# A gated attention and MLP mix on one Trainium2 core: another hand-written order of the attention, a shared PSUM pair for adjacent PV groups, and four small moves

## The chip, the cores and the metric

The kernel runs on one core of one Trainium2 chip. The metric is the device time of one execution in microseconds (us). The core has five engines that the text names as the profile does: TensorE (PE for its matmuls, PEld for its weight loads), VectorE (DVE), ScalarE (ACT), GpSimd (POOL) and SyncE (SP). Each works through its own queue in program order. DMAs are issued from the queues of SyncE and ScalarE here. Matmul results land in PSUM, which the kernel handles as banks of 128 x 512 float32 values, eight of them.

## The reference

The input x has 2048 rows of 512 values. Two branches work on it, and a gate mixes them:

```python
def _A_ref(x, wqkv, wo):                 # attention: 32 heads of 16, window of 256 keys
    qkv = (x @ wqkv) ...                 # q, k, v per head
    scores = einsum("bhqd,bhkd->bhqk", q, k) * (16 ** -0.5)
    mask = (q_index - k_index >= 0) & (q_index - k_index < 256)
    p = softmax(where(mask, scores, -1e9))
    return einsum("bhqk,bhkd->bhqd", p, v) ... @ wo

def _B_ref(x, w1, b1, w2, b2):           # channel MLP: 512 -> 1792 -> 512
    y = layernorm(x)
    h = gelu(y @ w1 + b1)
    return h @ w2 + b2

g = sigmoid((x * gate_w).sum(-1, keepdims=True))
out = g * _A_ref(x, ...) + (1 - g) * _B_ref(x, ...)
```

## The kernel before

Everything is float32. For the large products each operand is split into a rounded high part (type fp32r) and the rest, its low part; the product is then three matmuls, high times high, high times low and low times high. A high part is a copy or cast to fp32r (helper `copy` on ScalarE, line 131, or a VectorE `tensor_copy`), a low part is a subtraction (helper `lo_part`, line 128, on VectorE or GpSimd).

The kernel has three stages, one after the other on TensorE.

**Head and projections (to about 144 us).** `first_units` (line 259) computes the first q and k projection in four steps of 128 input values each. In a step both weight tiles, `ws[0]` and `ws[1]`, are cast to a high part and subtracted to a low part, the x chunk is split by `hi` and `lo`, and six matmuls (line 290) use them. `load_x(c)` (line 232) returns these helpers for one of the four chunks of x; `lo` uses VectorE for chunks 0 to 2 and GpSimd for chunk 3. Then a list of units follows (`qk_unit`, line 297, with its matmuls at line 303, and `v_unit`, line 326, matmuls at line 333), with a plan of what else is issued at which unit. q and k go to DRAM and come back as stacks of heads. The first rows of scores for the maxima (`s_pair`) run here too.

**Attention and the MLP's first layer (about 144 to 488 us).** Four kinds of work are woven together by the string ORDER, a letter at a time, in `run` (line 735):

- S (`s_pair`, line 348): two score matmuls (line 357) into a PSUM pair; VectorE masks them (line 366) and takes each row's maximum (line 367). After every fourth row block `put_max` (line 371) sends the maxima through DRAM into extra rows of the q stack. Its four steps run 6, 13, 19 and 28 letters after the S (`CHAIN`); the third, `put` (line 385), issues a DMA from ScalarE's queue, or from SyncE's for the maxima that are finished before ORDER starts.
- T (`st_pair`, line 403): two transposed score matmuls (line 412), which include the subtracted maximum; ScalarE takes the exponential (line 414) and GpSimd zeroes what the mask excludes (line 416).
- P (`pv`, line 423): up to 16 matmuls of a PV group (line 431) in four column tiles of 32, into the first bank of a PSUM pair. ScalarE copies the result out (VectorE once no S is left).
- f (`fill`, line 706): one step of the MLP's first layer (`mlp1_unit`, line 626): two matmuls (line 638) with 64 rows each. 24 steps make one unit, which holds one PSUM pair all that time; its two banks are copied out by ScalarE at the end.

The eight PSUM banks are four pairs, b0 to b3, in a list `ring`. `two` (line 112) takes the pair for the next T, S or P from it: the place in the list is a digit of the string PICK, 0 being the pair that was used longest ago. A pair may be written again when its last reader is done. After ORDER come six more fills, the last P and the remaining fills.

**Second layer and output (about 488 us to the end).** A loop over 4 chunks of 512 rows x 14 blocks of the hidden layer runs `mlp2` (line 851, matmuls at line 858), 12 matmuls a step. `attn_out(c)` (line 794) is called at step 4 for the first chunk and at step 11 of each chunk for the next one. With `after(k, ...)`, which puts work k steps later, it loads the attention's sums, takes reciprocals (line 810), loads the numerators and the reciprocals, and from the tenth step on scales one block of 128 rows a step (`scale`, line 815: a VectorE product at line 816, a high and a low part); a step later 12 matmuls (line 827) multiply it by wo.

Of the kernel before, what the change touches and what calls it, by code (L numbers as in the profile page):

```python
# [34 lines left out]
EPS = 1e-5  # L35
NEG = -3.0e38
U8 = mybir.dt.uint8
ORDER = ("TfSfSfffffTfSfffTSfffTfSfffTSfffTfSffSPTSffTfSfffTSfffSPSTfSfffTfSfTffTffTSffTfffTSPSSTPSTfTfffTSffT"
         "ffSffTSffffTSfffTfSffTfSfffSPSTSPTffSTffTfffTfSTffffTSffTfSfffTSfffTfSffSPSSTPTffTSffTffSffTfSfffTSf"
         "ffTfSfffTSfffTfSfSPSTTPTTSPSSTPSffTSffffSTfffTffSffTfSfffTfSffTfSfffSPSTTffffSTffTfffSTffTfffSSPfSfT"  # L40
         "ffSffTfTfffTSPSSTPTffTSfffTfSffTfSffffTSfffTfSffTffSffTPfSSPTffSfTfSffTfSfTffTffSTfffSffTfSfffTSfffS"
         "PTSTPSTSPTffTSffTffSffTSffffTSffffSTfffTffTfSfSfPSSTPfSfTfSfffTfTffSfTfSffffTSfffTfSffffTfSPSTSPTfSf"
         "ffTSfffTfSffTfSfffTfSfTfffTSfTffffTSPTTSPSTSPfTfSTfffSfffTSfffTfSffTfSfffTSfffTfSffSPPSTffTfffSTffTf"
         "ffTfSTfffSfTffTfSffTfSfffSPSSTPSffTfSfffTSfffTfSfffTSfffTfSfffTSffffSPPfSTfTfffSfTffTfSffTffTfSffTff"
         "SfTfTffffSPTTSPSTSPSfffTSfffTfSffTfSffffTSfffTfSffTfSfffSPfSTfTffffTfSTfffTfSfffTSfffTfSffTfSfffSPTS"
         "SPPTSTffffTfSTfffSffTfSfffTSfffTfSffTfffSfSPTSTPSSfTffffTfSffTfSfffTSfffTfSfffTSfffffSTPTTSPTSffTffS"
         "ffTfSfffTSfffTffSfTfTfffSTfTfffSPSSSPPSTSffffTfSfffTSfffTfTfffSTfffTffSTffffSPSTSPSTffTfffSTffTffTSf"
         "ffSffTSfffTfSffTfSfffSPSTSPfTfSTfffTffTSfffTfSfffTSfffTfSffTfSfffSPTTSPSTSPTffTSffTfSfffTfSfffSSfffT"
         "ffffTSffTfSffSPSffTSfffTfSffTfSffSTfffTffTffTfTffffTfPPTTTPfTffTffTffTPPTfTfffTffTfffTTffTfffTfPfTTf"
         "TTffffP")  # L50
PICK = ("0000000000000000001000000000000000000001000100100000000000000000100001000100000000000001000000000000"
        "0000000000000100010000010000000000001001001000101010001000100000000000000000001000000000100000000000"
        "0010000000000001000010020101010000000000100101000000000000000010000001000010000000000000000100100010"
        "1000000000100000000000000000000000000000000000000001000000000000000000010001000000000000001000000100"
        "0000000000000000100000000000000000000000000001001100000010010000000010010000000010000010000000000010"
        "00010000000000000000000101000100000100000000000000010000000000000000000000000000000")
LAG = 6
CHAIN = (6, 13, 19, 28)

# [2 lines left out]
def gated_mix_kernel(ctx, tc: tile.TileContext, xt, x2, wq0, wqk, wv, wo, xa, gw, w1, w2, b1, b2, out):  # L62
# [67 lines left out]
    def copy(dst, src):  # L130
        act.activation(dst, src, AF.Copy)  # L131
# [12 lines left out]
    spot = [None]  # L144
# [87 lines left out]
    def load_x(c):  # L232
        h, l = x8(), x8()
        xh.append(h)
        xl.append(l)
        raw = vs[:, 4 * c:4 * c + 4].rearrange("p b r -> p (b r)")
        for dt in range(DT):
            sp.dma_start(raw[:, dt * C:(dt + 1) * C], xt[c, :, dt * C:(dt + 1) * C])

        def part(t, dt):  # L240
            return t[:, dt * C:(dt + 1) * C]

        def hi(dt, eng=act):
            if eng is dve:
                dve.tensor_copy(part(h, dt), part(raw, dt))
            else:
                copy(part(h, dt), part(raw, dt))

        def lo(dt):
            lo_part(part(l, dt), part(raw, dt), part(h, dt), dve if c < 3 else pool)  # L250

        def rest():
            for dt in range(DT):
                hi(dt)
                lo(dt)

        return rest, hi, lo

    def first_units():
        ws, os = [], []  # L260
        for t in range(2):
            w = wt()
            wq[0, t] = w
            ws.append(w)
        raws = f32(get("work", "wv", DT, (128, 2, 512), F32R)).rearrange("p a (d t n) -> p (a d) t n", d=2, t=2)
        for a, b in ((0, 1), (1, 2), (2, 4)):
            act.dma_start(raws[:, a:b], wq0[:, a:b])
        _, hi, lo = load_x(0)
        idle = t2()
        dve.memset(idle[:, :256], 0.0)  # L270
        idle = idle.bitcast(BF16)
        o = two()[:, 0]
        for _ in range(10):
            pe.matmul(o, idle[:, :128], idle[:, :512], start=True, stop=True)
        loads()
        for t in range(2):
            os.append(ps("d"))
        for dt in range(DT):
            k = slice(dt * 128, dt * 128 + 128)
            if dt == 0:  # L280
                hi(dt, dve)
            for t in range(2):
                copy(ws[t][:, 0, k], raws[:, dt, t])
                lo_part(ws[t][:, 1, k], raws[:, dt, t], ws[t][:, 0, k])
                if dt and not t:
                    hi(dt)
            lo(dt)
            for n, (k, x) in enumerate(((0, xh[0]), (1, xh[0]), (0, xl[0]))):
                for t in range(2):
                    pe.matmul(os[t], ws[t][:, k, dt * 128:dt * 128 + 128], x[:, dt * C:dt * C + C],  # L290
                              start=dt == 0 and n == 0, stop=dt == DT - 1 and n == 2)
        rests[1]()
        rests[2]()
        for t in range(2):
            qk_out(0, t, 0, os[t])
# [75 lines left out]
    def put_max(p, a):  # L371
        mx = mxs[p][:, :, :, a:a + 4]
        m = small("nm", 2, (128, 2, 2, 2, 4), F32R)
        ms = small("ms", 2, (128, 32))
        md = dram.tile([2, 2, 2, 4, 128], F32R, name=nm("md"))

        def parts():
            pool.tensor_copy(m[:, 0], mx)
            lo_part(m[:, 1], mx, m[:, 0], pool)

        def turn():
            dve.transpose(ms, f32(m).rearrange("p a b c d -> p (a b c d)"))

        def put(eng=act):
            eng.dma_start(f32(view(md, [32, 4], [128, 32], [1, 32])), ms)

        def rest():
            done.add(("m", p, a // 4))
            for k in range(2):
                src = view(md, [512, 2], [1024, 2], [1, 512], off=2048 * k)  # L390
                sp.dma_start(f32(qk[62 + k:113 + k:50, :2, a * 128:a * 128 + 512]), f32(src))

        if spot[0] is None:
            parts()
            after(1, lambda: (turn(), put(sp)))
            after(3, rest)
        else:
            for n, fn in zip(CHAIN, (parts, turn, put, rest)):
                soon(n, fn)
# [19 lines left out]
    def flush():  # L419
        while late:  # L420
            late.pop(0)()

    def pv(p, j, last):
        flush()
        a = two()[:, 0]
        parts = ((-1, 0, 128, 256), (-2, 0, 256, 128), (0, 0, 0, 256), (1, 128, 0, 128))[0 if j else 2:]
        for n, (d, at, fr, w) in enumerate(parts):
            kb = 2 * j + d
            for h in range(4):
                v = (4 * p + h) * VW  # L430
                pe.matmul(a[32 * h:32 * h + 32, at:at + w], vs[:, kb, v:v + 32], pts[p, kb][:, h, fr:fr + w],  # L431
                          start=n == 0, stop=n == len(parts) - 1, skip_group_check=True, tile_position=(0, 32 * h))
        if j % 2 == 0:
            sums.append(sums.pop(0))
            acc[p] = sums[-1]
        s = acc[p]
        o = j % 2 * 256
        if last:
            dve.tensor_copy(s[:, o:o + 256], a[:, :256])
        else:  # L440
            copy(s[:, o:o + 256], a[:, :256])
        if j % 2:
            to = osc[p, :, (j - 1) * 256:(j + 1) * 256]
            if lt:
                after(1, lambda: sp.dma_start(to, s))
            else:
                act.dma_start(to, s)
# [287 lines left out]
    def run(order):  # L735
        for a in order:
            spot[0] += 1
            for fn in soons.pop(spot[0], []):
                fn()
            flush()  # L740
            if a == "T":
                p, kb, pr = lt.pop(0)
                if not pr:
                    block(p, kb)
                st_pair(p, kb, pr)
            elif a == "S":
                s_pair(*ls.pop(0))
            elif a == "P":
                pv(*lp.pop(0), not ls)
            else:  # L750
                fill()
# [42 lines left out]
    def attn_out(c):  # L794
# [49 lines left out]
                after(g, lambda g=g: load_o(g))  # L844
            after(4 + g, lambda g=g: load_r(g))
        for b in range(4):
            after(10 + b, lambda b=b: scale(b, *(t[:, :, b * 128:b * 128 + 128] for t in (o, r))))

    accs = {}

# [98 lines left out]
```

## Time and profile before

| what | value |
|---|---|
| median of 3 runs | 694.88 us |
| the three runs | 691.83, 694.88, 695.27 us |
| the profiled execution's own time | 691.57 us |
| its span (first to last instruction) | 689.8 us |
| granted TensorE clock | 1.00 |
| TensorE busy with matmuls | 681.9 us (99%) |
| VectorE, ScalarE, GpSimd busy | 474.1, 385.5, 267.2 us |

The profile is of one execution. The profiled execution's own time is 1.7 us more than its span. A row of the timeline reads: start in us, length in us, engine, line, operation, output <- input, shape, xcount, and in brackets the idle time of the engine before it with what ended it. In a group's row the numbers behind the bar are the busy time in us, the mean length of one in ns, and the idle time before them. A matmul's end is modelled; its start is not.

### The profile page before, as it was taken

The page shows a single profiled execution, that of the slowest core. Times are in us where ns is not written, and L with a number is a line of the kernel's source. Part 1 is how long each engine was busy: PE and PEld are TensorE (multiplying, and loading weights), DVE is VectorE, ACT ScalarE, POOL GpSimd, SP SyncE. Part 2 cuts the span into 40 slices and gives each one's busy share as a digit, 9 for nine tenths or more (in the row PEclk, how much of TensorE's full clock was granted, in tenths as well). Part 3 has the DMA queues.
Part 4 walks back from the last instruction along what each step waited for, and adds up shares of the span by engine and source line. Part 5 has one row for each costly group of instructions (what it writes and reads, how often), then busy time and mean ns, then how long its engine had stood idle before and what let it go on. Part 6 is the DMA issues. An engine that isn't in the chain of part 4 may idle for free.

```text
span 689.8 us, 15777 instructions
## 1 busy us (share of the span) xinstructions
PE 681.9 (99%) x5738; PEld 538.2 (78%) x5738; DVE 474.1 (69%) x971; ACT 385.5 (56%) x639; POOL 267.2 (39%) x623
## 2 busy tenths in 40 slices
PE   9999999999999999999999999999999999999997
PEld 6887777877877778778787877777787888888886
DVE  6646789966877878778587777866575555556444
ACT  6437454447677676876767767678633224123221
POOL 6900156426566664755666655558000000000000
PEclk9999999999999999999999999999999999999999
DMA  8998888785765668665776556436775450841801
GB/s 319 351 317 271 246 255 270 226 248 176 231 202 165 203 212 271 194 198 177 198 251 195 182 166 202 154 108 216 277 241 189 143 181 4 267 133 40 255 0 62
DMA packets 89621, 137.92 MB, mean 200 GB/s; under 512 B 13160, under 2 KB 36648, under 8 KB 89416
## 3 DMA queue, kind: packets, MB, share of 16 engines
q1 hardware_dynamic: 81120, 128.69, 58.4%
q10 hardware_dynamic: 8424, 8.23, 3.9%
q8 instruction: 46, 0.75, 0.5%
q14 instruction: 31, 0.25, 0.1%
HBM read 81.53 MB, written 54.30 MB: 197 GB/s over the span
## 4 chain that ended last, share of the span: by engine, by line
PE 86%; DMA 7%; POOL 3%; DVE 1%; ACT 1%; SPq 1%; issue 1%; ACTq 0%; DVEq 0%; POOLq 0%
PE ps_b L638 22%; PE ps_a L858 16%; PE ps_b L431 12%; PE ps_d L303 10%; PE ps_b L357 7%; PE ps_b L412 6%; PE ps_o L827 6%; PE ps_d L333 6%; DMA ra<-rd 1%; DMA hp<-t 1%; DMA t<-in_w 1%; DMA oa<-osc 1%; PE ps_x L357 1%; DMA wv<-in_wq 1%; POOL x L128 1%
## 5 line engine op out<-in xcount | busy, mean ns | idle before, releaser
L638 PE MATMUL ps_b<-x,w 64*128 64x512 f32 x1344 | 211.1, 395 | 0.2 <-ACT pb L414 0.2
L858 PE MATMUL ps_a<-x,t 128*128 128x512 f32 x648 | 149.6, 389 | 0.0
L367 DVE TENSOR_REDUCE mx<-ps_b 128x2 f32<-128x512 f32 x208 | 144.1, 693 | 7.2
L858 PEld LDWEIGHTS ps_a<-x,t 128*128 128x128 f32 x648 | 121.6, 188 | 25.3
L638 PEld LDWEIGHTS ps_b<-x,w 64*128 64x128 f32 x1344 | 130.0, 186 | 10.6 <-issue 2.0
L366 DVE COPY_PREDICATED ps_b<-tri,ps_b 128x256 f32<-128x256 uint8 x208 | 88.3, 424 | 44.0 <-PE ps_b L357 32.7
L416 POOL TENSOR_SCALAR_AFFINE_SELECT pa<-pa 128x256 f32<-128x256 f32 x192 | 73.9, 412 | 68.6 <-ACT pa L414 67.9
L414 ACT ACTIVATE pa<-ps_b 128x768 f32<-128x768 f32 x96 | 76.5, 813 | 25.6 <-PE ps_b L412 18.8
L412 PE MATMUL ps_b<-qk 64*128 64x384 f32 (+5 forms) x512 | 88.8, 336 | 0.4 <-ACT pb L414 0.3
L303 PE MATMUL ps_d<-x,w 128*128 128x512 f32 x360 | 85.1, 391 | 0.1
L357 PE MATMUL ps_b<-qk 62*128 62x384 f32 (+3 forms) x472 | 83.2, 345 | 0.8 <-ACT t L131 0.6
L303 PEld LDWEIGHTS ps_d<-x,w 128*128 128x128 f32 x360 | 67.2, 188 | 15.1 <-POOL x L128 0.5
L416 POOL TENSOR_SCALAR_AFFINE_SELECT pb<-pb 128x256 f32<-128x256 f32 x160 | 62.4, 417 | 39.2 <-ACT pb L414 38.5
L414 ACT ACTIVATE pb<-ps_b 128x768 f32<-128x768 f32 (+2 forms) x96 | 65.6, 706 | 16.8 <-PE ps_b L412 12.5
L412 PEld LDWEIGHTS ps_b<-qk 64*128 64x128 f32 (+1 forms) x512 | 50.8, 184 | 15.7 <-issue 4.0
L694 ACT ACTIVATE t<-t,b1s 128x512 f32<-128x512 f32 x56 | 38.5, 716 | 43.4 <-DMA t<-hp 42.8
L416 POOL TENSOR_SCALAR_AFFINE_SELECT x<-x 128x256 f32<-128x256 f32 x128 | 49.7, 417 | 25.8 <-ACT x L414 25.4
L357 PEld LDWEIGHTS ps_b<-qk 62*128 62x128 f32 (+1 forms) x472 | 45.4, 184 | 17.4 <-issue 3.8
L414 ACT ACTIVATE x<-ps_b 128x768 f32<-128x768 f32 x64 | 51.2, 813 | 13.0 <-PE ps_b L412 10.4
L827 PE MATMUL ps_o<-w,t 128*128 128x512 f32 x192 | 46.3, 390 | 1.0 <-ACT t L131 1.0
L333 PE MATMUL ps_d<-wv,x 128*128 128x512 f32 x192 | 46.7, 394 | 0.0
L431 PE MATMUL ps_b<-pa,v 128*32 128x256 f32 (+1 forms) x768 | 43.3, 330 | 0.2 <-POOL x L416 0.2
(96 smaller groups left out, 757.1 us busy)
## 6 DMA issues: line engine op xcount, KB each, us to landing
qk<-qk SPq DMA_DIRECT2D x112, 196.0 KB
t<-hp SPq DMA_DIRECT2D x56, 256.0 KB
hp<-t SPq DMA_DIRECT2D x54, 256.0 KB
qk<-t SPq DMA_DIRECT2D x48, 256.0 KB
osc<-x SPq DMA_DIRECT2D x31, 256.0 KB
t<-in_w SPq DMA_DIRECT2D x28, 256.0 KB
w<-w SPq DMA_DIRECT2D x28, 256.0 KB
qk<-t ACTq DMA_DIRECT2D x24, 256.0 KB
```

The costliest lines, as they stand in the source:

```text
L303: pe.matmul(o, a[:, dt * 128:(dt + 1) * 128], b[:, dt * C:(dt + 1) * C], start=n == 0, stop=n == 11)
L333: pe.matmul(o, x[:, a:a + 128], wvs[dt][:, k], start=n == 0, stop=n == 11)
L357: pe.matmul(o[:, e, :n], qs[pr][r:k, qb * 128:qb * 128 + 128], ks[pr][r:k, t0:t0 + n], start=True, stop=True)
L366: dve.copy_predicated(o[:, :, :128], tri, o[:, :, 256:384])
L367: dve.tensor_reduce(m, o[:, :, :256], mybir.AxisListType.X, ALU.max)
L412: pe.matmul(o[:, e, :w], ks[pr][r:k, kb * 128:kb * 128 + 128], qs[pr][r:k, kb * 128:kb * 128 + w], start=True, stop=True)
L414: act.activation(pt[:, :, :w], o[:, :, :w], AF.Exp, scale=0.25)
L416: pool.affine_select(out=pt[:, :, a:a + 128], in_=pt[:, :, a:a + 128], pattern=[[0, 2], [sgn, 128]], base=b, channel_multiplier=-sgn, comp ...
L431: pe.matmul(a[32 * h:32 * h + 32, at:at + w], vs[:, kb, v:v + 32], pts[p, kb][:, h, fr:fr + w], start=n == 0, stop=n == len(parts) - 1, sk ...
L638: pe.matmul(o[:, e], w[kt // 4][r:r + 64, k, m:m + 128], y[r:r + 64, a:a + C], start=n == 0, stop=n == 23)
L827: pe.matmul(a, x[:, g], wos[g][:, k], start=n == 0, stop=n == 11)
L858: pe.matmul(accs[c][b], x[:, b * 128:(b + 1) * 128], w, start=f == 0 and n == 0, stop=f == FT - 1 and n == 2)
```

## The change

Six edits:

- ORDER and PICK are replaced. The new ORDER has the same 256 T, 236 S and 63 P, and 647 f in place of 652; PICK has 575 digits in place of 583.
- `pv` takes a PSUM pair by `two` only if it has none open: a P right behind another P uses the second bank of the same pair. Any other letter between them closes the pair.
- `attn_out` starts its scaling at step 12 in place of 10 for the first chunk; the other chunks keep 10.
- In `first_units` the second weights' high parts of steps two to four are cast by VectorE, ahead of the step's other work, and no longer by ScalarE.
- The low parts of x chunk 3 are computed by VectorE for its last two tiles; GpSimd keeps the first two.
- `put` issues its DMA from SyncE's queue while the letter count `spot[0]` is at most 99, and from ScalarE's after that.

```diff
-ORDER = ("TfSfSfffffTfSfffTSfffTfSfffTSfffTfSffSPTSffTfSfffTSfffSPSTfSfffTfSfTffTffTSffTfffTSPSSTPSTfTfffTSffT"
...
-         "ffffTSffTfSffSPSffTSfffTfSffTfSffSTfffTffTffTfTffffTfPPTTTPfTffTffTffTPPTfTfffTffTfffTTffTfffTfPfTTf"
-         "TTffffP")
+ORDER = ("TfSfSfffffTSffffTSfffTfSfffTSfffTfSffSPTSffTSffTfSffTffSffSPSTfffTSffTffTfSfTfffTfSPSTSPSTfTfffTSfff"
...
+         "fSffTfSffTSfffSPSffTSffffTSfffTfSffSfTfffTffTffTPfTfTTffPPTfTfTfffTffTfPfTTPTfTffTfTffTffffTPPTfTfTf"
+         "fT")
...
         def lo(dt):
-            lo_part(part(l, dt), part(raw, dt), part(h, dt), dve if c < 3 else pool)
+            lo_part(part(l, dt), part(raw, dt), part(h, dt), dve if c < 3 or dt > 1 else pool)
...
             if dt == 0:
                 hi(dt, dve)
+            else:
+                dve.tensor_copy(ws[1][:, 0, k], raws[:, dt, 1])
             for t in range(2):
-                copy(ws[t][:, 0, k], raws[:, dt, t])
+                if not dt or not t:
+                    copy(ws[t][:, 0, k], raws[:, dt, t])
                 lo_part(ws[t][:, 1, k], raws[:, dt, t], ws[t][:, 0, k])
...
-        def put(eng=act):
-            eng.dma_start(f32(view(md, [32, 4], [128, 32], [1, 32])), ms)
+        def put(eng=None):
+            (eng or (act if spot[0] > 99 else sp)).dma_start(f32(view(md, [32, 4], [128, 32], [1, 32])), ms)
...
+    pair = [None]
+
     def pv(p, j, last):
         flush()
-        a = two()[:, 0]
+        if pair[0] is None:
+            pair[0] = two()
+            a = pair[0][:, 0]
+        else:
+            a = pair[0][:, 1]
+            pair[0] = None
...
             flush()
+            if a != "P":
+                pair[0] = None
             if a == "T":
...
-            after(10 + b, lambda b=b: scale(b, *(t[:, :, b * 128:b * 128 + 128] for t in (o, r))))
+            after((10 if c else 12) + b, lambda b=b: scale(b, *(t[:, :, b * 128:b * 128 + 128] for t in (o, r))))
```

More of the change, by code (lines that the diff above doesn't have):

```diff
@@ L37 @@
 U8 = mybir.dt.uint8
-ORDER = ("TfSfSfffffTfSfffTSfffTfSfffTSfffTfSffSPTSffTfSfffTSfffSPSTfSfffTfSfTffTffTSffTfffTSPSSTPSTfTfffTSffT"
[L39 to L48, printed above, removed]
-         "ffffTSffTfSffSPSffTSfffTfSffTfSffSTfffTffTffTfTffffTfPPTTTPfTffTffTffTPPTfTfffTffTfffTTffTfffTfPfTTf"
-         "TTffffP")
@@ L51 @@
[L51 to L56, printed above, removed]
+ORDER = ("TfSfSfffffTSffffTSfffTfSfffTSfffTfSffSPTSffTSffTfSffTffSffSPSTfffTSffTffTfSfTfffTfSPSTSPSTfTfffTSfff"
+         "TfSffTfSfffTSfffTfSffTfSfffSPSTSPTffSTffTfffTfSTffffTSffTfSfffTSfffTfSffSPSSTPTffTSffTffSffTfSfffTSf"
+         "ffTfSfffTSfffTfSfSPTSTPTTSPSSTPSffTSffffSTffffTfSffTfSfffTSfffTfSfffSPSTTffffSTfffTffSTffTfffSSPfSfT"
+         "ffSffTfTfffTSPSSTPTffTSffTffSffTfSfffTSfffTfSffTfSffTffSfSPPSTffTfSffTffTSfffTffSfTffSffTfSfffTSfffS"
+         "PTSTPSSTPTffTSffTffSffTfSfffTSfffTfSfffTTfffSfSfPSSTPfTffSTfTffSffTfSfffTSfffTfSfffSTffffTfSPSTSPfTf"
+         "SffTfSfffTSfffTfSfffSfTffTfSfTfffTfSPTSTPSSTPSffTSfffTfTffSfTffSfffTSffffTSfffTffSfSPPTSffSffTffTfff"
+         "STffTfffTfSTffTfSffTfSfffSPSSTPfTfSfffTSfffTfSffTfSfffTSffffSTffffSfSPPfSTfTfffSfTffTfSffTffSffTfffT"
+         "SffTfffTfSPTSTPSSTPSffTfSfffTfSffTfSffffTSfffTfSffTfSfffSPfSTfTffffTfSTfffTfSfffTSfffTfSffTfSfffSPTS"
+         "SPPTSTffffTfSTfffSffTfSfffTSfffTfSffTfffSfSPTSTPSSfTffffTfSffTfSfffTSfffTfSfffSTfffffTSPTTSPTSffTffS"
+         "ffTSffffTSfffTffSfTfTfffSTfTfffSPSSSPPSfTSffffTSfffTfSffTffTffSTfffTffSTffffSPSTSPSTffTfffSTffTffTSf"
+         "ffSffTfSffTfSffTfSfffSPSTSPTffSTffTfffTSffTffSffTSffffTSfffTfSfffSPTSTPSSTPTffTSffTfSfffTfSfffTSfffT"
+         "fSffTfSffTSfffSPSffTSffffTSfffTfSffSfTfffTffTffTPfTfTTffPPTfTfTfffTffTfPfTTPTfTffTfTffTffffTPPTfTfTf"
+         "fT")
@@ new lines @@
+PICK = ("0000000000000000001000000000000000000001001000100000000000000000100001000100000000000001000000000000"
+        "0000000000000100010000010000000000001001001000101010001000100000000000000000000000000000000000000000"
+        "0010000000000000000100201001000000000100100101000000000000000100000001000000010000000000000100100010"
+        "0000000010000000000001000000000000000000010000000100000000000000000010001000000000000000000001000000"
+        "0000000000001000000000100100000000000000010011000000000000000001001000000001000001000000000001000010"
+        "000000000000000000201000100000000000000000000001000000000000000000000000000")
```

## The prediction

> **What bounds the kernel now.** I read the page's first part, then the busy time of each engine by stretch, then the list of what TensorE waited for, and only then the timeline around each wait.
>
> ```profile
> span 689.8 us, 15777 instructions
> ...
> PE 681.9 (99%) x5738; PEld 538.2 (78%) x5738; DVE 474.1 (69%) x971; ACT 385.5 (56%) x639; POOL 267.2 (39%) x623
> ```
>
> ```profile
> 144.50:488.00 343.50, 341.98 (x4248) 264.57 (x4248) 260.46 (x586) 249.87 (x384) 209.69 (x552) 1.00 0.62 195
> 488.00:689.80 201.80, 196.94 (x870) 162.15 (x866) 109.79 (x190) 62.60 (x98) 0.00 (x0) 1.00 0.47 151
> ```
>
> ```profile
> PE ps_x L274 <- DVE t L270: 1.3, 1, 1.3
> PE ps_o L827 <- ACT t L131: 1.0, 1, 1.0
> PE ps_b L357 <- ACT t L131: 0.6, 1, 0.6
> ```
>
> In the stretch rows the columns are length, then busy time of PE, PEld, DVE, ACT and POOL, the granted clock, the DMA share and GB/s. TensorE is busy 99% of the span at a granted clock of 1.00, and nothing else is over 78%. So a change that leaves the matmuls alone can earn only what TensorE loses. The wait list shows how little that is: a few single waits of at most 1.3 us. A matmul's end is modelled, though, and a short wait can hide under it, so I also measured waits from start to start. The yardstick is the steady rate, here from the chain of waits:
>
> ```profile
> 533.63 2.72 PE ps_a L858 x12
> ```
>
> Twelve matmuls of 512 columns start in 2.72 us, 0.227 us each. The diff leaves the number and shape of the matmuls as they are, so the forecast is a sum of small losses removed, against new ones.
>
> **The head: the second weights' high parts go from ScalarE to VectorE.** The first projection runs four steps of six matmuls (L290).
>
> ```profile
> 5.60 6.10 PE L290 MATMUL ps_d<-x,w 128*128 128x512 f32 x24
> 11.54 11.04 PE L303 MATMUL ps_d<-x,w 128*128 128x512 f32 x48
> ```
>
> ```profile
> 5.02 0.43 DVE L245 CAST x<-v 128x512 fp32r<-128x512 f32 x1 [3.82 <-DMA v<-in_xt]
> ...
> 6.97 0.30 ACT L131 ACTIVATE w<-wv 128x128 fp32r<-128x128 f32 x1
> 7.30 0.29 DVE L128 TENSOR_TENSOR w<-wv,w 128x128 fp32r<-128x128 f32 x1 [0.43 <-ACT w L131]
> 7.50 0.69 DVE L128 TENSOR_TENSOR x<-v,x 128x512 fp32r<-128x512 f32 x1
> ...
> 8.24 0.99 PEld L290 LDWEIGHTS ps_d<-x,w 128*128 128x128 f32 x5 [0.34 <-DVE x L128]
> ```
>
> From 5.60 to 11.54 is 5.94 us, where 24 x 0.227 = 5.44 would do: 0.50 us lost. At the second step VectorE idles 0.43 us until ScalarE has cast the second weights (6.97), so its low part of x, started at 7.50, ends at 8.19 and the weight load has waited 0.34 us for it. After the change VectorE casts these weights itself, ahead of its subtractions, in steps two to four; ScalarE sheds three times 0.30 us. The trace has no 128x128 cast on VectorE. From above it is bounded by the 0.43 us cast of 512 columns; the 0.29 us subtraction of the same tile is nearest, and below zero it cannot be. I take 0.25. VectorE's step then is 0.25 + 2 x 0.29 + 0.69 = 1.5 us by durations, somewhat less by starts (its instructions overlap: 7.30 to 7.50 is 0.20), against TensorE's 6 x 0.227 = 1.36: about level. So the 0.34 us wait should go, less what later steps give back. Term: 0.2 us saved, bounds 0.4 saved to 0.3 lost. If VectorE is the slower of the two, the subtractions for the next x chunks queue behind it; they have no consumer before L303 at 11.54.
>
> **Two of the four low parts of the last x chunk go from GpSimd to VectorE.**
>
> ```profile
> 25.09 5.49 POOL L128 TENSOR_TENSOR x<-v,x 128x512 fp32r<-128x512 f32 x4 [1.11 <-ACT x L131]
> ...
> 28.71 0.72 DVE L128 TENSOR_TENSOR w<-t,w 128x512 fp32r<-128x512 f32 x1 [3.10 <-ACT w L131]
> ...
> 30.64 2.40 PEld L303 LDWEIGHTS ps_d<-x,w 128*128 128x128 f32 x11 [0.55 <-POOL x L128]
> ```
>
> ```profile
> 27.86 6.06 PE L303 MATMUL ps_d<-x,w 128*128 128x512 f32 x24
> 33.76 5.60 PE L333 MATMUL ps_d<-wv,x 128*128 128x512 f32 x24
> ```
>
> From 27.86 to 33.76 is 5.90 us for 24 matmuls, 0.46 over 5.44, and the weight load names its cause: GpSimd's fourth subtraction, ending at 30.58. VectorE is idle from 25.61 to 28.71, so two subtractions of 0.69 us (the 7.50 row) fit; the last of the four then lands two GpSimd turns (2 x 1.37) earlier. Saved: 0.45 us. It costs nothing, because the 3.10 us idle covers 1.4; without that cover the weights' low part at 28.71 would be late by what is over.
>
> **Two early hand-overs of the row maxima go from ScalarE's queue to SyncE's.** put_max writes 16 KB to DRAM; in the run of ORDER it was issued by ScalarE. With the new test only those up to spot 99 change queue. The chain puts an issue 19 spots after its S, and by the new string only spots 37 and 75 qualify: two of 30.
>
> ```profile
> L385 ACTq DMA_DIRECT2D md<-ms x30: 510/518/1048, 152.9 to 461.6; - x30
> ```
>
> ```profile
> 152.93 1.05 ACTq L385 DMA_DIRECT2D md<-ms  x1
> ...
> 154.08 1.08 ACT L131 ACTIVATE t<-ps_b 128x512 f32<-128x512 f32 x2 [0.87 <-DMA md<-ms]
> ...
> 154.17 0.44 PE L412 MATMUL ps_b<-qk 64*128 64x384 f32 x2
> ...
> 154.70 2.56 SPq L651 DMA_DIRECT2D hp<-t  x2
> ...
> 155.22 0.44 PE L357 MATMUL ps_b<-qk 62*128 62x384 f32 x2 [0.60 <-ACT t L131]
> ```
>
> The first is the longest of all 30 (1048 ns against a median of 518) and sits in front of the two copies that empty the MLP bank pair. TensorE starts a T pair at 154.17 and the next S at 155.22: 1.05 us, where a T lasts 0.17 (next part), so 0.88 lost. Issued by SyncE, behind which only the hp writes of 154.70 are queued, and they wait for those copies anyway, the copies start up to 0.87 us earlier. What is next is the copies' own 1.08 us: started near 153.2 they end before the S. Saved: 0.85 us; 0 if the new order brings another wait to the same place.
>
> **The order.** Both strings hold 256 T, 236 S and 63 P; the fills fall from 652 to 647, and five more run after the last P. What a run of P costs at its edge:
>
> ```profile
> 165.73 0.35 PE L412 MATMUL ps_b<-qk 64*128 64x384 f32 x2
> 165.90 0.35 PE L357 MATMUL ps_b<-qk 62*128 62x384 f32 x2
> 166.18 0.64 PE L431 MATMUL ps_b<-pa,v 128*32 128x256 f32 x8
> ```
>
> T to S takes 0.17 us, S to P 0.28: 0.11 at the way in, and I take the same for the way out (bounds 0 to 0.2). The strings have 57 and 56 runs of P, seven pairs of adjacent P in place of six: one run fewer, 0.2 us. Sharing one bank pair spares seven choices of a bank, which matters only where a bank is late.
>
> The old string ends with T after T:
>
> ```profile
> 478.45 0.22 PE L412 MATMUL ps_b<-qk 64*128 64x128 f32 x2
> 479.01 0.33 PE L412 MATMUL ps_b<-qk 64*128 64x128 f32 x2 [0.34 <-ACT pb L414]
> 479.50 1.20 PE L638 MATMUL ps_b<-x,w 64*128 64x512 f32 x8 [0.16 <-ACT pb L414]
> ```
>
> Two T pairs of 128 columns take 1.05 us, where a third of 0.17 each, 0.11 in all, would do: 0.94 lost, waiting for exponentials that free the banks. The new string ends "TPPTfTfTfT": the last four T stand apart by a fill, and the six fills after them cover the last exponentials. Saved: 0.9 us, bounds 0.9 to 0.3. The many other short waits of the stage fall anew; I take them as equal, give or take 1.5 us.
>
> **Later first scaling.** The first output chunk's scale moves two steps of 2.72 us down.
>
> ```profile
> 524.88 0.95 DVE L810 RECIPROCAL su<-su 128x128 f32<-128x128 f32 x1 [6.51 <-DMA su<-osc]
> ...
> 526.76 2.48 DVE L866 TENSOR_TENSOR us<-ps_a,b2s 128x512 f32<-128x512 f32 x4
> ...
> 529.15 0.69 DVE L816 TENSOR_TENSOR oa<-oa,ra 128x512 f32<-128x512 f32 x1
> ...
> 530.62 3.01 PE L827 MATMUL ps_o<-w,t 128*128 128x512 f32 x12 [1.00 <-ACT t L131]
> ```
>
> VectorE stood 6.51 us before the reciprocal of the next chunk, so the four bias additions ran late and the scaling behind them at 529.15; TensorE waited 1.00 us for its cast. Two steps later there are 5.44 us of cover. The outputs of the chunk leave 5.4 us later, and nothing in the second chunk's steps needs their buffer. Saved: 1.0 us.
>
> **The sum.** 0.2 + 0.45 + 0.85 + 0.2 + 0.9 + 1.0 = 3.6 us. The profiled execution took 691.57 us (span 689.8), so it would become 688.0. The runs took 691.83, 694.88 and 695.27: with the profiled one two near 691.7 and two near 695.1, and nothing in one trace says what parts them. I set the sum against the mean of the four, 693.4, and forecast a median of 689.8 us.
>
> **The rivals.** *The waits move instead of going.* A bank pair is free again only when its reader is done:
>
> ```profile
> L367 DVE TENSOR_REDUCE mx<-ps_b 128x2 f32<-128x512 f32 x208 | 144.1, 693 | 7.2
> ...
> L366 DVE COPY_PREDICATED ps_b<-tri,ps_b 128x256 f32<-128x256 uint8 x208 | 88.3, 424 | 44.0 <-PE ps_b L357 32.7
> ...
> L414 ACT ACTIVATE pa<-ps_b 128x768 f32<-128x768 f32 x96 | 76.5, 813 | 25.6 <-PE ps_b L412 18.8 <-POOL pa L416 2.5 <-POOL x L416 1.1
> ```
>
> After an S that takes 0.42 + 0.69 = 1.1 us, after a T 0.81. For it: counted along the two strings, the places where the same pair comes round within about such a time are 18 and 19, as many as before, and within the first 70 letters, where the 0.85 us sits, they are four in place of two. Against it: the three waits with names outside the attention (0.45, 1.0 and 0.2) do not depend on the string. Then 1.95 us of order and queue are given back: 693.4 - 1.65 = about 691.8, and with another 1.5 us of new short waits 693.3. Chance 0.27.
>
> *Sharing the bank pair serialises the two PV groups.* If the second group has to wait until the first group's half has been copied out, TensorE stands at each of the seven pairs for the copy, and for the exponentials that are ahead of it on ScalarE:
>
> ```profile
> L131 ACT ACTIVATE x<-ps_b 128x256 f32<-128x256 f32 x56 | 21.6, 385 | 29.9 <-PE ps_b L431 27.3 <-ACT t L131 1.1 <-DMA qk<-qk 0.9
> ```
>
> That is 0.385 us alone, 1.2 behind one exponential of 0.81, 2.0 behind two. At 1.4 a pair it costs 9.8, and the result is 693.4 - 3.6 + 9.8 = 699.6; it decides for slower by over 0.5% (698.4) from 1.25 us a pair. For it: no row shows TensorE writing one half of such a tile while ScalarE reads the other. Against it: the halves lie 512 f32 columns apart, and the groups touch no element in common. Chance 0.08. The Trainium skill, page "PSUM — Partial Sum Buffer", section "PSUM bank collisions raise a hardware error", asks for a guard by bank and quadrant, not by tile, and gives a bank 512 f32 values; by that rule the halves are two banks, the wait is not needed, and the sum stays 3.6. No run here shows it yet.
>
> *Nothing reaches the clock*: the terms are right but the median falls among the upper runs, 695.1 - 3.6 = 691.5. This lies at the edge of the bound below and is counted half to each side.
>
> **How the numbers follow.** A measurement of this kernel can tell about 0.5%, 3.5 us, from no change: faster is under 691.4. The forecast case has 0.65, of which a little falls above 691.4; the moved waits 0.27, a part of it under; the serialised pairs 0.08, nearly all slower. So faster 0.60, same 0.33, slower 0.07. Low end: all terms at their best, 1.5 us from the other short waits and a lower-run median, 691.7 - 5.2 = 686.5. High end: the moved waits with new ones and some more, 694.3.
>
> **What would show it.** Right: no wait of TensorE named ACT t L131 at the output projection nor of POOL x L128 at L303; the 24 matmuls of L290 within 5.75 us start to start; no ACTq L385 before 170 us and T to S near 154 us in 0.2 us; the last T pairs 0.3 us apart or less; attention 1.5 to 2.5 us shorter. Wrong: in a pair of P, an idle TensorE before the second group released by ACT x L131; or new waits over 0.3 us in the attention, by ACT exponentials or by the DMA of the row maxima, that sum to 2 us.

## The result, and the profile after

The changed kernel is slower: 698.99 us against 692.82 us in the median of seven runs each. These medians lie 6.2 us apart; the ratio over the runs is 1.0081 with a 95% interval of 1.0060 to 1.0102, some 5.6 us. The forecast was 689.8 us. The profiled execution took 697.72 us, its span is 696.0, against 691.57 and 689.8.

The page's first lines of the changed kernel:

```profile
span 696.0 us, 15788 instructions
...
PE 681.9 (98%) x5738; PEld 538.5 (77%) x5738; DVE 475.6 (68%) x976; ACT 385.7 (55%) x636; POOL 262.5 (38%) x621
```

The matmuls' busy time is the same 681.9 us to the tenth; all 6.2 us of the span are time in which TensorE did nothing. The list of what TensorE waited for says for whom (us in total, times, longest):

```profile
PE ps_b L441 <- ACT x L131: 2.7, 5, 0.7
PE ps_b L415 <- DMA qk<-md: 2.0, 1, 2.0
PE ps_x L274 <- DVE t L270: 1.3, 1, 1.3
PE ps_b L441 <- DVE x L449: 1.1, 2, 0.5
PE ps_b L360 <- ACT pb L417: 0.9, 1, 0.9
PE ps_d L293 <- ACT w L131: 0.5, 1, 0.5
PE ps_x L360 <- DVE mx L370: 0.4, 1, 0.4
...
PE ps_x L360 <- DVE mx L366: 0.2, 1, 0.2
```

The two large waits of before are gone (ACT t L131 at the output projection and at S). In their place stand seven waits of the PV line for the copy of a PV result, and one of T for the read-back of the row maxima. The 0.5 us at L293, in the head, is no new loss: the matmuls ahead of it end sooner in this execution, and the first projection starts at 5.59 us, as it did at 5.60 before. By stage, in the stretches from the first T to the first step of the second layer and from there to the end, first before, then changed:

```profile
144.70:488.50 343.80, 342.28 (x4250) 264.71 (x4249) 260.89 (x588) 249.87 (x384) 209.69 (x552) 1.00 0.62 195
488.50:689.80 201.30, 196.44 (x866) 162.00 (x864) 109.36 (x187) 62.60 (x98) 0.00 (x0) 1.00 0.47 150
```

```profile
145.30:495.80 350.50, 342.85 (x4249) 264.93 (x4248) 258.65 (x583) 250.88 (x384) 208.16 (x552) 1.00 0.62 193
495.80:696.00 200.20, 196.27 (x866) 162.00 (x864) 111.14 (x193) 62.71 (x98) 0.00 (x0) 1.00 0.47 150
```

The attention is 6.7 us longer, the last stage 1.1 shorter, and the first T starts 0.6 us later in spite of the head's moves. The timeline of the changed kernel at its first shared pair shows the new wait:

```profile
243.54 0.86 PE L441 MATMUL ps_b<-pa,v 128*32 128x256 f32 x16
244.45 0.38 ACT L131 ACTIVATE x<-ps_b 128x256 f32<-128x256 f32 x1
244.89 0.86 PE L441 MATMUL ps_b<-pa,v 128*32 128x256 f32 x16 [0.49 <-ACT x L131]
```

The second group starts when ScalarE has copied out the first, at 244.83, although it writes the other bank. The trace also keeps which semaphore an instruction waits for: the second group's first weight load, at 244.89, waits for ScalarE's, which the copy raises. So the wait stands in the program. Start to start such a pair loses 0.55 to 0.74 us over the steady rate of a run of P; the seven make about 4.4 us.

### The profile page after: what moved, and what is told of

The parts are those of the page before. It is cut to its first block, busy times and chain, and to the rows that moved or that the text cites. A ratio compares the mean times of both kernels' runs of the same rounds, so it can differ in the third digit from the quotient of the medians.

```text
span 696.0 us, 15788 instructions
## 1 busy us (share of the span) xinstructions
PE 681.9 (98%) x5738; PEld 538.5 (77%) x5738; DVE 475.6 (68%) x976; ACT 385.7 (55%) x636; POOL 262.5 (38%) x621
## 4 chain that ended last, share of the span: by engine, by line
PE 81%; DMA 7%; DVE 4%; ACT 3%; issue 2%; SPq 2%; POOL 1%; ACTq 0%; DVEq 0%
PE ps_a L870 22%; PE ps_b L648 22%; PE ps_b L441 12%; PE ps_b L415 7%; PE ps_b L360 6%; PE ps_o L839 6%; PE ps_d L306 4%; PE ps_d L336 2%; DMA t<-in_x 2%; DMA qk<-qk 1%; DMA qk<-t 1%; DMA gws<-in_gw 1%; ACT t L131 1%; DMA md<-ms 1%; DVE x L128 1%
## 5 line engine op out<-in xcount | busy, mean ns | idle before, releaser
L648 PE MATMUL ps_b<-x,w 64*128 64x512 f32 x1344 | 211.2, 395 | 0.2
L648 PEld LDWEIGHTS ps_b<-x,w 64*128 64x128 f32 x1344 | 130.2, 186 | 9.7 <-issue 1.6
L415 PE MATMUL ps_b<-qk 50*128 50x384 f32 (+5 forms) x512 | 90.1, 339 | 2.0 <-DMA qk<-md 2.0
```

The source lines that it names most:

```text
L415: pe.matmul(o[:, e, :w], ks[pr][r:k, kb * 128:kb * 128 + 128], qs[pr][r:k, kb * 128:kb * 128 + w], start=True, stop=True)
L648: pe.matmul(o[:, e], w[kt // 4][r:r + 64, k, m:m + 128], y[r:r + 64, a:a + C], start=n == 0, stop=n == 23)
```

## The experiments

Theory P: the shared pair makes the second group wait for the first group's copy, and this costs over 4 us. Rival O: the new order is what is slow, and the pair only shows it. All ratios are to the kernel before.

### Unshared, and shared with a later copy

The first kernel undoes the sharing alone; the second keeps it, and issues the first copy after the second group's matmuls (both edits shortened).

```diff
-        if pair[0] is None:
-            pair[0] = two()
-            a = pair[0][:, 0]
-        else:
-            a = pair[0][:, 1]
-            pair[0] = None
+        a = two()[:, 0]
```

> The changed kernel with one edit undone: every PV group takes a bank pair of its own again (PICK gets a 0, the oldest pair, where a second P now chooses). Theory P (the shared pair makes the second group wait for the copy of the first): the eight groups of matmuls after a shared first half no longer lose their 0.55 to 0.74 us each, 4.4 us in all; against the kernel before the ratio falls from 1.008 to about 1.002, and no wait of TensorE at the PV line is released by ACT x L131 for over 0.3 us inside a run of P. Rival O (the order itself is slower, the pair only shows it): the wait turns up at the next letter that needs a bank, and the ratio stays within 1.006 to 1.010.

```diff
+        held_out.append(out)                       # out(): the copy and, for odd j, the store
+        if pair[0] is None or ahead[0] != "P":     # ahead: the next letter of ORDER
+            while held_out:
+                held_out.pop(0)()
```

> The changed kernel with the pair still shared, but the copy of the first half is issued after the matmuls of the second group. Theory P: the second group has nothing to wait for, 4.4 us are saved and the ratio to the kernel before is about 1.002, as in the unpaired kernel; ScalarE's first copy may now end up to 1.4 us later, which delays an exponential behind it by nothing much. Rival O: ratio 1.006 to 1.010. A third view, that the two halves of a pair cannot be written and read at once for a reason of the chip: then the second group loses nothing but the copies stretch, and the gain is under 2 us.

Measured: 1.0019 (1.0001 to 1.0036) unshared and 1.0018 (0.9995 to 1.0040) with the later copy, from 1.0081. Both take away about 4.3 us, near the sum of the losses at the seven pairs (the expectation says eight groups; there are seven). The timeline of the kernel with the later copy, at the same pair:

```profile
242.64 1.51 PE L442 MATMUL ps_b<-pa,v 128*32 128x256 f32 x32
...
244.86 0.66 ACT L131 ACTIVATE x<-ps_b 128x256 f32<-128x256 f32 x2 [1.29 <-PE ps_b L442]
```

The groups now run through, both copies follow them, and no weight load of the second group waits for ScalarE's semaphore. Theory P holds, and its size within the intervals. One of the seven pairs brings nothing, though: the last run of P takes 3.41 us from its first to its last matmul in the changed kernel, 3.40 unshared and 3.45 with the later copy, because a wait for GpSimd's masks comes in place of the one that goes. What stays open is whether ScalarE can read one bank of the pair while TensorE writes the other: here both copies come after the second group, so no run shows it.

### The sharing in the old order

```diff
     (the kernel before, with the sharing of pv and run as changed,
      and PICK without the six digits that it spares)
```

> The kernel before with the sharing alone: its own order, in which six P follow a P directly, and the digits of PICK that these six no longer need taken out. If the wait at a shared pair is a matter of the pair and not of the new order, each of the six second groups loses about 0.62 us, 3.7 us in all: ratio about 1.0054, and the wait list shows the PV line released by the copy of the first group. Rival (the pair costs only where the new order has ScalarE busy): under 1.5 us, ratio 1.002 or less.

Measured: 1.0061 (1.0037 to 1.0085), 4.2 us for six pairs. The wait list:

```profile
PE ps_b L438 <- ACT x L131: 2.2, 4, 0.7
...
PE ps_b L438 <- DVE x L446: 1.1, 2, 0.5
```

Four for ScalarE's copy, two for VectorE's at the end, where it does the copying. So the cost comes with the pair in the old order too.

### The small moves without the order, and the order without them

```diff
     e4: ORDER, PICK and pv of before, the other four edits as changed
     e3: ORDER, PICK and pv as changed, the other four edits undone
```

> The kernel before with the four small moves alone, its own ORDER and PICK and no sharing. By the prediction's terms 2.5 us faster than before, ratio 0.9964. Rival: they bring new waits for VectorE's maxima in the projections, about 0.95 us, and the gain is at most 1.5 us, ratio 0.998 or more.

> The changed kernel with the four small moves undone (second weights' cast back on ScalarE, low parts of the last chunk on GpSimd, first scaling at step 10, put always on ScalarE's queue): order and pair alone. By the prediction's terms the small moves are worth 0.2 + 0.45 + 0.85 + 1.0 = 2.5 us, so this is 2.5 us slower than the changed kernel, ratio about 1.012. Rival: the new waits of 0.95 us for VectorE's maxima at 55 and 99 us come from the small moves, and the put's 0.85 is no longer there to be lost; then this is at most 0.7 us slower than the changed kernel, ratio 1.008 to 1.009.

Measured: 0.9963 (0.9947 to 0.9978) for the small moves alone, 2.6 us faster, as the prediction's terms say; this kernel beats both. Order and sharing alone: 1.0091 (1.0070 to 1.0113). Against the whole change, 1.0081, the small moves are then worth 0.7 us in the new order, with intervals too wide to tell this from 2.6. Between the unshared kernel and the small moves alone lies what the new order costs by itself: 1.0019 over 0.9963, 3.9 us, give or take 1.6. So the 5.6 us are -2.6 from the small moves, +3.9 from the order and +4.3 from the sharing; these are steps from one kernel to the next, so their sum is no check of its own.

In words, the edits of the small moves one by one, on the kernel before:

```diff
     e9:  put from SyncE's queue up to spot 99
     e10: scaling at step 12 for the first chunk
     e11: second weights' cast and two low parts to VectorE
```

> The kernel before with one small move: the two early hand-overs of row maxima issued by SyncE. The prediction's term is 0.85 us: ratio 0.9988, the wait of 0.77 us at 154 us gone from the trace. Rival: what the copies gain there is lost at the next bank within some us; ratio 1.000.

> The kernel before with the later first scaling alone. The prediction's term is 1.0 us: ratio 0.9986, no wait of TensorE for ACT t L131 at the output projection. If the spread between executions of the kernel before (691 to 697 us) comes from that stage, the gain in the runs is larger than in one trace, 2 us or more: ratio 0.997. Rival: another wait of the same stage (low parts of the hidden block on VectorE) takes its place, ratio 0.9995 or more.

> The kernel before with the two moves of the head alone (second weights' cast and two low parts to VectorE). By the prediction's terms 0.65 us: ratio 0.9991. By the traces so far nothing: TensorE comes to the S pair near 98 us earlier by that much and waits for VectorE, whose maximum ends at the same time as before (98.9 us); the first T starts at 144.7 us as before; ratio 1.000.

Measured: 0.9981 (0.9967 to 0.9995) for the queue, 1.3 us; 0.9991 (0.9978 to 1.0004) for the scaling, 0.6 us; 0.9994 (0.9978 to 1.0009) for the head, 0.4 us. Only the first is clear of 1, but their sum, 2.3 us, fits the 2.6 together. What the head saves is lost in part before the first T. Where it goes is in the timelines around 99 us, first of the kernel before, then of the kernel with the head's moves alone:

```profile
98.23 0.69 DVE L367 TENSOR_REDUCE mx<-ps_x 128x2 f32<-128x512 f32 x1
...
98.85 0.65 PE L357 MATMUL ps_x<-qk 62*128 62x384 f32 x4
```

```profile
98.55 0.44 PE L360 MATMUL ps_x<-qk 62*128 62x384 f32 x2
98.77 0.69 DVE L370 TENSOR_REDUCE mx<-ps_x 128x2 f32<-128x512 f32 x1
...
99.60 0.44 PE L360 MATMUL ps_x<-qk 62*128 62x384 f32 x2 [0.61 <-DVE mx L370]
```

TensorE comes 0.3 us earlier and waits 0.61 us at the second S for VectorE, which here is no earlier, but half a microsecond later; why it is later these rows do not show. VectorE sets the time at this place in this execution, and the first T then starts at 145.3 us against 144.8 before, where the expectation had it unmoved. Over all traces: four of the nine kernels with the head's moves start the first T at 145.3 to 145.8, the other five at 144.5 to 144.7; the five kernels without them start it at 144.6 to 145.1. So at the first T no gain of the head is to be seen, and the 0.6 us by which the changed kernel's first T is late lies within what executions differ by.

### The order's largest wait: the read-back of the maxima

The wait of 2.0 us for "DMA qk<-md" stands in each kernel so far with the new order (1.9 to 2.4 us). The timelines, changed kernel and then before:

```profile
273.94 0.53 ACTq L388 DMA_DIRECT2D md<-ms  x1
...
275.02 1.62 SPq L347 DMA_DIRECT2D qk<-qk  x2
...
279.66 1.28 SPq L394 DMA_DIRECT2D qk<-md  x2
...
282.37 0.44 PE L415 MATMUL ps_b<-qk 64*128 64x384 f32 x2 [1.99 <-DMA qk<-md]
```

```profile
272.20 0.52 ACTq L385 DMA_DIRECT2D md<-ms  x1
...
275.88 1.28 SPq L391 DMA_DIRECT2D qk<-md  x2
277.25 1.81 SPq L344 DMA_DIRECT2D qk<-qk  x4
```

SyncE waits for the write before it issues the read-back. From the write's issue to the read-back's it is 5.7 us after the change and 3.7 before; and the new order puts a load of stacks between them, because T and its block come ahead of the letter at which the read-back is due. Two edits of the unshared kernel:

```diff
-            for n, fn in zip(CHAIN, (parts, turn, put, rest)):
+            for n, fn in zip((3, 8, 12, 28) if (p, a) == (3, 4) else CHAIN, (parts, turn, put, rest)):
```

> The unpaired kernel (changed kernel, each PV group with its own bank pair), with one hand-over of row maxima brought forward: for pass 3, row blocks 4 to 7, the chain runs 3, 8 and 12 letters after the S in place of 6, 13 and 19; its last step stays at 28. In every kernel with the new order TensorE waits 2.0 to 2.6 us near 280 us for the read-back of these maxima. Theory M1 (the write of the maxima is issued too late): with the write 7 letters, about 2 us, earlier the wait falls to under 0.5 us and the ratio to the kernel before goes from 1.002 to about 0.999. Theory M2 (the write lands late because a load of stacks goes out between it and its read-back): the landing comes earlier too, since the write is then ahead of that load, so the wait goes as well. Rival: the maxima are not what delays TensorE there; the ratio stays 1.002 and another wait stands in the same place.

```diff
-            if not kb and p:
+            if not kb and p == 3:
+                after(2, lambda: load_stacks(p, S - 256, 256))
+            elif not kb and p:
                 load_stacks(p, S - 256, 256)
```

> The unpaired kernel, with the write of the maxima left at its place, but the load of the last 256 columns of the stacks of pass 3, which the new order issues between that write and its read-back, put one key block later (its first reader comes over 7 us after the load). Theory M2: the landing of the write takes 3.7 us again, as in the kernel before, in place of 5.7, and TensorE's wait of 2.0 to 2.6 us falls under 0.5 us; ratio about 0.999. Theory M1: the landing and the wait stay, 2 us or more; ratio 1.002.

Measured: 0.9990 (0.9968 to 1.0011) with the write earlier, 0.9993 (0.9973 to 1.0012) with the load later, both from 1.0019, with intervals that overlap its own (1.0001 to 1.0036). The traces say more. The wait list of the first no longer has the maxima among TensorE's waits:

```profile
PE ps_x L274 <- DVE t L270: 1.3, 1, 1.3
PE ps_b L360 <- ACT pb L417: 0.6, 1, 0.6
PE ps_b L436 <- POOL x L419: 0.5, 2, 0.3
```

So by the medians the late maxima are 2.0 us of the order's 3.9, within the intervals. By the profiled executions they are nearly all of it: from the first T to the second layer the small moves alone take 343.6 us, the unshared kernel 346.1, which is 2.5 more with a wait of 2.2 us for the maxima in it, and with the write earlier it is 344.5. The second edit shortens the wait, but does not end it:

```profile
PE ps_b L415 <- DMA qk<-md: 2.2, 3, 1.3
PE ps_b L360 <- ACT pb L417: 2.1, 1, 2.1
```

The same hand-over in its timeline:

```profile
275.56 0.53 ACTq L388 DMA_DIRECT2D md<-ms  x1
...
280.34 1.27 SPq L394 DMA_DIRECT2D qk<-md  x2
```

The longest, 1.3 us, is the one near 283 us, in place of 2.0 or more; the two others are for other maxima, at 216 and 476 us, and the wait of 2.1 us is at 254 us. This profile is of the slowest of the kernel's twelve executions (696.05 us, median 692.21), so its other waits prove little. From write to read-back it is 4.8 us; theory M2 said 3.7, and that was wrong. The other traces place it: in the eight kernels in which no load of stacks goes out between the two and SyncE waits for this write, it is 3.6 to 4.8 us; in the four with the load, 5.2 to 5.9. So within the new order the load goes with a landing that is later by 0.4 to 1.1 us, and is part of the cause. The other part, as the first edit shows, is that the write is issued late for the T that needs it.

### The new end, and an earlier chain for all

```diff
     e8: the small moves alone, with the last 54 letters of the new ORDER, and there
-    TffffTPPTfTfTffT
+    TffTffPPTfTfTffT
```

> The kernel before with the four small moves and the new order's last 54 letters alone (unshared pairs), in which two fills are moved from before the last T ahead of the final PP to behind it, so that the PV group no longer waits for GpSimd's masking of that T. The old end loses 0.94 us in T after T; the new end loses 0.73 us in that PV group instead in each kernel that has it. With both gone: 0.9 us less than the small moves alone, ratio about 0.995 against 0.9963. Rival: the wait moves to the next P or to the last fills, and the ratio stays at 0.9963.

Measured: 0.9984 (0.9968 to 0.9999), where the same moves with the old end gave 0.9963 (0.9947 to 0.9978). The 0.9 us did not come. That the new end is worse is not shown either: the intervals overlap, and from the first T to the second layer, the stretch that holds the edit, the two profiled executions take 344.0 and 343.6 us. The T after T is gone, but the last run of P takes 3.36 us from its first to its last matmul, where the other runs of 64 matmuls in this trace take 2.54. Its timeline shows what it waits for:

```profile
476.73 1.54 ACT L417 ACTIVATE x<-ps_b 128x768 f32<-128x768 f32 x2
...
477.21 1.94 POOL L419 TENSOR_SCALAR_AFFINE_SELECT pb<-pb 128x256 f32<-128x256 f32 x4
...
479.10 1.49 POOL L419 TENSOR_SCALAR_AFFINE_SELECT x<-x 128x256 f32<-128x256 f32 x4
...
480.28 0.41 PE L434 MATMUL ps_b<-x,v 128*32 128x128 f32 x4 [0.31 <-POOL x L419]
```

GpSimd begins with the tile's masks only at 479.10, 0.83 us after the exponentials are done (478.27), because it is still at the masks of the tile before. Two fills are too few for that queue. My expectation was wrong there.

```diff
     e12: the small moves alone, and
-CHAIN = (6, 13, 19, 28)
+CHAIN = (4, 9, 14, 28)
```

> The kernel before with the four small moves, and with all hand-overs of row maxima brought forward: the chain runs 4, 9 and 14 letters after its S in place of 6, 13 and 19, its last step stays at 28. If late read-backs of the maxima are part of what lengthens some executions, this is 0.3 to 1 us faster than the small moves alone, ratio 0.995 to 0.996 and a smaller spread of the runs. Rival: ScalarE now waits in its queue for the transposes, ahead of exponentials, and the ratio rises to 0.998 or more.

Measured: 1.0033 (1.0015 to 1.0050), the rival's side and more: 4.8 us given away against 0.9963. From the first T to the second layer the profiled execution takes 347.6 us against 343.6. The wait list has new entries for VectorE's maxima:

```profile
PE ps_b L415 <- DVE mx L366: 0.8, 2, 0.5
...
PE ps_b L360 <- DVE mx L370: 0.4, 1, 0.4
```

These make 1.2 us of the 4.8. So setting all steps of the chain earlier costs more than one late read-back; where the rest is lost, and in which queue, I did not test.

## Why the prediction was wrong, step by step

Forecast and measurement lie 9.2 us apart. Of this, 4.3 us are the sharing, which the sum put at nothing, and 5.0 us the order, which was to save 1.1 (0.2 and 0.9) and costs 3.9. The small moves came out as summed, 2.6 against 2.5 us, in the old order.

**Sharing the pair: wrong, and the largest term.** The sum had nothing for it; "the sum stays 3.6" rested on the two halves having no element in common, and on a rule of the chip taken for one of the program. The Trainium skill, page "PSUM — Partial Sum Buffer", section "PSUM bank collisions raise a hardware error", asks for a guard by bank and quadrant, and says that by bank is the simple version. No run here tests this rule. It says what the chip needs, not what the program waits for, and this program has the wait. The rival that describes it got 0.08. The sharing measured 4.3 us, 0.62 a pair, less than the 1.4 I took for the rival and nearer to the copy alone (0.385); the 1.25 us from which the rival alone was to decide was not reached.

**"The many other short waits of the stage fall anew; I take them as equal, give or take 1.5 us": wrong.** The new order by itself costs 3.9 us, of which 2.0 are the read-back of the maxima. I counted bank pairs in the strings, but not the letters between the read-back and the T that needs it, nor what SyncE issues between. The prediction names this wait among the signs of being wrong, with no price. The other 1.9 us are not placed; with the intervals they may be anything from nothing to about 4, and the profiled executions show only 0.3 of them in this stage.

**The end of the order: seen rightly, and given back at another place.** The last T pairs no longer wait, which is the 0.94 us; in the changed kernel's timeline TensorE's fills (L648) lie between them:

```profile
487.44 0.24 PE L415 MATMUL ps_b<-qk 64*128 64x128 f32 x2
487.50 0.70 PE L648 MATMUL ps_b<-x,w 64*128 64x512 f32 x4
488.01 0.25 PE L415 MATMUL ps_b<-qk 64*128 64x128 f32 x2
```

But the last run of P ahead of them takes 3.4 us where 2.5 would do. In the changed kernel its second group waits for the copy of the first, which VectorE does here:

```profile
485.08 0.64 PE L441 MATMUL ps_b<-pa,v 128*32 128x256 f32 x8 [0.55 <-DVE x L449]
```

Without the sharing the same run waits for GpSimd's masks instead, as long. (The string ends in TPPTfTfTffT; the prediction dropped one f.)

**The put: right.** 1.3 us against 0.85 in the old order, with an interval of 0.3 to 2.3. In the new order:

```profile
153.53 0.60 SPq L388 DMA_DIRECT2D md<-ms  x1
...
154.80 0.44 PE L415 MATMUL ps_b<-qk 64*128 64x384 f32 x2
...
155.05 0.41 PE L360 MATMUL ps_b<-qk 62*128 62x384 f32 x2
...
156.55 0.44 PE L360 MATMUL ps_b<-qk 62*128 62x384 f32 x2 [0.31 <-ACT pa L417]
```

T to S is 0.25 us in place of 1.05, as forecast; it is 0.24 to 0.27 in all nine traces with this move and 1.01 to 1.05 in the five without. The next S waits for ScalarE's exponentials, 0.65 us from T to S, but it does so in the new order without the move as well, so nothing is given back there.

**The head and the low parts: right where they are, lost on the way.** The changed kernel's timeline:

```profile
6.52 0.22 DVE L283 CAST w<-wv 128x128 fp32r<-128x128 f32 x1
...
27.67 5.60 PE L306 MATMUL ps_d<-x,w 128*128 128x512 f32 x24
33.11 1.07 PE L336 MATMUL ps_d<-wv,x 128*128 128x512 f32 x4
```

The cast takes 0.22 us (0.25 was taken), and the second 24 matmuls take 5.44 us start to start, the 0.46 is gone. The first 24 take 5.77 in place of 5.94, near the 0.2 of the sum, though executions differ by more: 5.8 to 6.2 in the nine traces with this move, 5.9 to 6.4 in the five without. The cost to VectorE was taken too low: its two subtractions were to fit as 2 x 0.69 us, and took 2.56 (0.86 and 1.77, with an overlap) of the 3.10 us that were idle before. The long one ran beside one of GpSimd:

```profile
26.02 1.74 POOL L128 TENSOR_TENSOR x<-v,x 128x512 fp32r<-128x512 f32 x1
...
26.53 1.77 DVE L128 TENSOR_TENSOR x<-v,x 128x512 fp32r<-128x512 f32 x1
```

And "it costs nothing" looked only at the next consumer: at 55 and 99 us TensorE now waits for VectorE's maxima, and the first T comes no earlier. Such a wait stands in five of the nine traces with the head's moves and in none of the five without. The loss of 0.46 us also differs between executions: without the moves it is 0.5, 0.4, 0.1 and 0 us in the four other traces, and with them 0 in all nine. The term of 0.65 measured 0.4 with an interval that holds zero.

**The later scaling: right in kind, its size open.** No wait at the output projection for ScalarE's cast is left in any of the nine traces with the move; of the five without it four have one, of 0.6 to 1.2 us, and one has none. Alone the move measured 0.6 us in the runs, with an interval that holds zero. The 1.1 us by which the changed kernel's last stage is shorter is no better proof: that stage takes 200.1 to 202.1 us with the move and 200.1 to 202.7 without.

## What to carry to other kernels

Before two pieces of work share one buffer object, look in the program, not in the chip's rules, for a wait between the second piece and the reader of the first; if there is one, issue the reader after both. A reordered program has to be checked against every chain that crosses queues, DMAs above all: count the letters from a hand-over to its consumer and what else is issued in between. And a gain ahead of a stage that another engine sets is no gain; ask at each later meeting point who comes last.

## What the runs showed of the hardware that I had not expected

From the issue of the small write of the maxima to DRAM to the issue of the read-back that waits for it were 3.6 to 4.8 us where no load of stacks went out between them, and 5.2 to 5.9 where one did (twelve traces, the hand-over near 273 us); how much of this is the write's own landing the timelines do not separate.

Where VectorE and GpSimd subtracted at the same time, both were slower. In the changed kernel GpSimd's subtraction from 26.02 us and VectorE's from 26.53 overlap for 1.2 us and take 1.74 and 1.77 us; GpSimd's before it, at 24.76, took 1.30, and VectorE's of the same form took 0.69 in the head of the kernel before. Spans on GpSimd are rough, and no run here shows what the two share.
